# T5-bias attention with a snake MLP: output products and attention numerators in 64-row mode, tail keys by two pairs, one division per pair

## The chip, the core and the metric

The kernel runs on one core of a Trainium2 chip. The core has five engines with queues of their own: PE (TensorE, matmuls), DVE (VectorE), ACT (ScalarE), POOL (GpSimd) and SP (SyncE, which only issues DMAs here). The metric is the time on the device in microseconds (us); less is better.

## What is computed

Eight batches t of eight heads attend over 576 positions of width 64, with a bias that depends on the distance of two positions. The result, 4608 rows of 512, goes through an MLP of width 2048 with a sine in it. The reference, cut to its core:

```python
scores = scale * np.matmul(q, k.transpose(0, 1, 3, 2)) + bias      # (8, 8, 576, 576)
attn = np.exp(scores - max); attn = attn / (attn.sum(-1) + 1e-09)
x = np.matmul(attn, v)                                             # -> (4608, 512)
h = x @ w_in; s = np.sin(alpha * h)                                # (4608, 2048)
out = (h + s * s / alpha) @ w_out                                  # (4608, 512)
```

## The kernel before

**Attention.** The heads are taken in pairs p of two, with head a of a pair in partitions 64a to 64a+63, so that a score matmul uses half of PE's rows and the two heads' matmuls, which follow each other, use different halves (the 64-row mode, "rows" in the code). A pair's 576 keys are four chunks ch of 128 and a tail of 64; its 576 queries are five groups j of 128, the last half empty. qk_t (L1063) makes the scores of 256 queries w with two key chunks: four matmuls of 256 columns into two PSUM banks, and exp_u (L1074) turns them into numerators in one 1024-wide activation. qk_x_rows (L1055) does the last 64 queries with the four chunks, in rows; qk_x_full (L1051) and qk_s (L1038) do the tail keys with full 128-row matmuls, through tail (L1026), from a copy of k in which the two heads stand on a diagonal. DVE multiplies the exponentials by exp(bias) near the diagonal (band_t L1086, band_x L1078, band_s L1046).

**Numerators.** av (L1099) multiplies the exponentials by v with a column of ones, in full 128-row mode: for each j one tail matmul of 130 columns for both heads (L1111), then eight of 65 columns (four chunks for each head, L1120). It is called twice for a pair (two j, then three), each time with one bank, and each time norm (L1124) divides: a reciprocal (L1130) and a multiplication (L1131) on DVE. Then the pair's x is transposed, by a DMA on SP (turn_x L1135) or for the first pairs on PE (turn_x_pe L1141).

**The MLP.** It runs in nine blocks of rows. A unit is one block with one of 16 slices f of the width: moe_in (L1151) does four matmuls, moe_sin (L1168) a sine on ACT, moe_sq (L1173) and moe_g (L1176) a square and h + s*s/alpha on DVE. The output products, moe_out (L1192), take 128 rows tau at a time: 16 matmuls of 512 columns in full mode, two to a piece, into one bank; evict (L1201) and store (L1205) follow.

**What sets the order.** The whole order is laid out when the program is built. _graph (L333) makes tasks with an engine, a duration, a priority and what they depend on; _Plan.run (L177) goes through time, gives each free engine the ready task with the lowest priority number, hands out the eight PSUM banks (_Banks.find, L76) and adds 0.096 us (SWITCH, L121) where PE's mode changes between tasks. The program then issues each engine's instructions in the order found. At run time an engine goes through its own list strictly in order and waits at an instruction whose input isn't there. Scores and moe_in stand in one sequence ("big"), which the option ins fills with units; OPT holds these options, priorities p_... and buffer counts.

## Time and profile before

| | before |
|---|---|
| median of 2 runs | 396.99 us (394.71 and 399.26) |
| span of the profiled execution | 391.7 us |
| PE busy | 374.0 us (95%) |
| DVE busy | 301.1 us (77%) |
| ACT busy | 279.8 us (71%) |
| POOL busy | 86.4 us (22%) |

The profile doesn't say which of the runs it comes from. Its span runs from the first to the last instruction; the lower of the two times is 3.0 us above it and the upper one 7.6 us. "PE" in the profile is matmuls, "PEld" the loads of their stationary operand, which go on beside them. A matmul's row gives its start and its whole duration; since matmuls follow each other before the last one has ended, what one costs is read from start to start, or from the chain of waits, whose pieces follow each other without overlap.

### The profile page before, as it was taken

The numbers are of one execution on the slowest core, as the hardware profiler recorded it, in microseconds if no ns is written. First come the engines' busy times: TensorE is split into PE (matmuls) and PEld (weight loads), VectorE is DVE, ScalarE is ACT, GpSimd is POOL, SyncE is SP. The second block draws the span as 40 slices with busy tenths as digits, with TensorE's granted clock in tenths as the row PEclk, the third lists the DMA queues.
The fourth block names the chain that finished last, engine by engine and source line by source line (L and its number), as shares of the span: only waits on it lengthen the run. The fifth ranks groups of instructions, "written<-read, shape, count | busy, mean of one in ns | idle before, by whom it ended". The sixth has DMA issues, their size and how long they took to land.

```text
span 391.7 us, 9363 instructions
## 1 busy us (share of the span) xinstructions
PE 374.0 (95%) x3811; PEld 201.1 (51%) x3811; DVE 301.1 (77%) x738; ACT 279.8 (71%) x339; POOL 86.4 (22%) x101
## 2 busy tenths in 40 slices
PE   3979979999999999999999999999999999999996
PEld 2557435565446545564466445644664454444442
DVE  6498797777987798769976997798669889778221
ACT  2888876989689978887789769987897964333000
POOL 8695744080008000900080004000000000000000
PEclk9999998999999999999999999999999999999999
DMA  9999999999549924997499329600211001101122
GB/s 165 197 170 183 195 184 149 145 170 165 82 97 168 176 14 91 165 167 57 89 179 153 34 66 204 74 19 28 64 44 42 30 19 46 36 27 56 54 82 80
DMA packets 148171, 40.80 MB, mean 104 GB/s; under 512 B 134416, under 2 KB 143456, under 8 KB 148128
## 3 DMA queue, kind: packets, MB, share of 16 engines
q0 software_dynamic: 96656, 18.45, 57.7%
q1 hardware_dynamic: 50912, 21.25, 27.9%
q8 instruction: 30, 0.49, 0.5%
q10 hardware_dynamic: 560, 0.50, 0.4%
q14 instruction: 13, 0.11, 0.1%
HBM read 36.94 MB, written 15.93 MB: 135 GB/s over the span
## 4 chain that ended last, share of the span: by engine, by line
PE 88%; DVE 8%; DMA 2%; ACT 1%; issue 1%; SPq 0%
PE acc L1197 33%; PE acc L1163 29%; PE acc L1120 9%; PE acc L1069 9%; DVE g L1188 3%; PE acc L1111 2%; PE acc L1030 2%; PE acc L1059 2%; DMA toep<-in_k_dram 2%; DVE u L1097 1%; DVE s L1174 1%; PE acc L1010 1%; PE acc L1035 1%; DVE xp L1131 1%; DVE qT L1020 1%
## 5 line engine op out<-in xcount | busy, mean ns | idle before, releaser
L1076 ACT ACTIVATE u<-acc 128x1024 f16<-128x1024 f32 x160 | 154.4, 1024 | 21.2 <-PE acc L1069 9.7
L1197 PE MATMUL acc<-w_out,g 128*128 128x512 f16 x576 | 142.9, 381 | 0.0
L1163 PE MATMUL acc<-xT,w_in 128*128 128x512 f16 (+2 forms) x640 | 131.5, 358 | 0.0
L1170 ACT ACTIVATE s<-acc,alphaT 128x512 f16<-128x512 f32 (+2 forms) x144 | 96.2, 687 | 48.5 <-DVE g L1188 26.7
L1188 DVE SCALAR_TENSOR_TENSOR g<-s,inv_a,acc 128x512 f16<-128x512 f16 (+4 forms) x176 | 106.1, 643 | 1.6
L1163 PEld LDWEIGHTS <-w_in 128*128 128x128 f16 x640 | 58.8, 98 | 66.6 <-DVE g L1188 1.4
L1197 PEld LDWEIGHTS <-g 128*128 128x128 f16 x576 | 50.1, 98 | 56.0 <-issue 9.2
L1097 DVE TENSOR_TENSOR u<-u,toep 128x256 f16<-128x256 f16 (+1 forms) x128 | 61.0, 489 | 19.2 <-ACT u L1076 19.0
L1174 DVE TENSOR_TENSOR s<-s 128x512 f16<-128x512 f16 (+2 forms) x144 | 55.5, 417 | 6.1 <-ACT s L1170 6.1
L890 POOL DMA_DIRECT2D v<-in_v_dram x32 | 28.4, 900 | 143.6 <-PE acc L1120 135.8
L1120 PE MATMUL acc<-v,u 128*128 128x65 f16 x1280 | 54.6, 193 | 1.2 <-DVE u L1097 1.2
L1120 PEld LDWEIGHTS <-u 128*128 128x128 f16 x1280 | 50.0, 97 | 5.5 <-DVE u L1097 1.7
L1069 PE MATMUL acc<-qT,kT 64*128 64x256 f16 x512 | 45.1, 280 | 2.4 <-DVE g L1188 1.9
L1203 DVE COPY outs<-acc 128x512 f32<-128x512 f32 x36 | 24.7, 687 | 22.6 <-PE acc L1197 22.3
L1131 DVE TENSOR_TENSOR xp<-acc,rden 128x256 f16<-128x256 f32 (+1 forms) x64 | 31.4, 491 | 2.4 <-DVE rden L1130 0.3
L1069 PEld LDWEIGHTS <-kT 64*128 64x128 f16 x512 | 19.1, 96 | 24.6 <-issue 21.7
L1130 DVE RECIPROCAL rden<-acc 128x4 f32<-128x4 f32 (+1 forms) x64 | 12.0, 187 | 21.5 <-PE acc L1120 21.1
L1111 PE MATMUL acc<-vt,u 128*128 128x130 f16 x128 | 28.2, 221 | 0.0
L1111 PEld LDWEIGHTS <-u 128*128 128x128 f16 x128 | 12.5, 97 | 5.9 <-issue 2.1
L911 POOL DMA_DIRECT2D staged_q<-in_q_dram x5 | 13.9, 2783 | 0.0
L911 POOL DMA_DIRECT2D staged_k<-in_k_dram x6 | 13.6, 2259 | 0.7 <-DMA xT<-in_q_dram 0.7
L1059 PE MATMUL acc<-qT,kT 64*128 64x64 f16 x256 | 9.6, 195 | 2.8 <-ACT u L1076 0.9
(61 smaller groups left out, 166.6 us busy)
## 6 DMA issues: line engine op xcount, KB each, us to landing
out_dram<-outs SPq DMA_DIRECT2D x36, 256.0 KB, 2.0
v<-in_v_dram POOLq DMA_DIRECT2D x32, 128.0 KB, 6.7
staged_k<-in_k_dram POOLq DMA_DIRECT2D x6, 576.0 KB, 11.4
staged_q<-in_q_dram POOLq DMA_DIRECT2D x5, 576.0 KB, 15.4
w_in<-in_moe_w_in_dram POOLq DMA_DIRECT2D x4, 512.0 KB, 8.8
w_out<-in_moe_w_out_dram POOLq DMA_DIRECT2D x4, 512.0 KB, 9.6
xT<-in_q_dram POOLq DMA_DIRECT2D x11, 144.0 KB, 7.0
xT<-in_k_dram POOLq DMA_DIRECT2D x7, 144.0 KB, 6.2
```

Source lines behind the costliest of these rows:

```text
L890: self.nc.gpsimd.dma_start(out=self.vs[t % 2][:, c, :, 0:D], in_=src)
L1069: self.nc.tensor.matmul(out=s[:, o:o + 256], lhsT=self.kT[t % 2][r, p, 128 * c:128 * c + 128], rhs=self.qT[t % 2][r, p, 256 * w:256 * w + ...
L1076: self.nc.scalar.activation(out=c["u"], in_=c["s"], func=AF.Exp, scale=0.125)
L1097: self.nc.vector.tensor_tensor(out=io, in0=io, in1=m, op=ALU.mult)
L1111: nc.tensor.matmul(out=c["av"][:, 130 * j:130 * j + 130], lhsT=tail, rhs=vt[:, p, :], start=True, stop=True, skip_group_check=True)
L1120: nc.tensor.matmul(out=c["av"][:, 130 * j + 65 * a:130 * j + 65 * a + 65], lhsT=l, rhs=vv[:, ch, 2 * p + a, 0:65], start=False, stop=True, ...
L1131: self.nc.vector.tensor_tensor(out=self.ap(x, 256 * w, [[64, n], [1, 64]]), in0=self.ap(av, 0, [[65, n], [1, 64]]), in1=self.ap(r, 0, [[1, ...
L1163: self.nc.tensor.matmul(out=c["h"][:, x:y], lhsT=self.w_in[:, j, 128 * f:128 * f + 128], rhs=self.xT[:, j, lo + x:lo + y], start=(j == 0), ...
L1170: self.nc.scalar.activation(out=c["s"], in_=c["h"], func=AF.Sin, scale=self.alphaT[:, f:f + 1])
L1174: self.nc.vector.tensor_tensor(out=c["s"], in0=c["s"], in1=c["s"], op=ALU.mult)
L1188: self.nc.vector.scalar_tensor_tensor(out=o, in0=c["s"][:, x:y], scalar=self.inv_a[:, f:f + 1], in1=c["h"][:, x:y], op0=ALU.mult, op1=ALU.add)
L1197: self.nc.tensor.matmul(out=c["mo"], lhsT=self.g[b][:, f, 128 * (tau % 4):128 * (tau % 4) + 128], rhs=self.w_out[:, f, :], start=(f == 0), ...
```

## The change

- **Numerators** (batches 2 to 7): a pair's five j are done by one set of tasks into two banks, one for each head. If PE is in 64-row mode when the first piece comes, each 128-row matmul is cut into two of 64 rows (av_rows). In turn 0, head 0 takes the first 64 partitions (keys) of each chunk and head 1 the last 64; in turn 1 the halves are swapped. Between the turns stands touch, a DVE copy of one element from each of the two banks: it reads after the last matmul of turn 0 and turn 1 waits for it. If PE is in full mode, the pieces are done in full mode without a touch.
- **Output products**: two groups of 128 rows are taken together, into two banks; each slice f is done in full mode or as two half matmuls with the turns, whichever mode PE is in, and a touch stands between the turns there too. An odd group is done alone in full mode.
- **Tail keys and last queries**: the tail keys of two pairs make one tile (L, four a batch becoming two) of full-mode matmuls of 512 columns; the last queries of two pairs make one tile (R) in rows; each has one band multiplication.
- **Division**: one reciprocal and one multiplication for each pair (norm_pair) instead of two each.
- **Planner and options**: a task may have a gate, which settles its mode and duration when it is chosen. Scores of batches 2 to 7 get two pairs of banks (low=4) in place of three, in a written order for each batch. Priorities, load order, the place of the first MLP units (ins) and buffer counts are new. One more pair is transposed on PE. Batches 0 and 1 keep the old functions for scores and numerators.

The core of the diff:

```diff
+                    if t.gate is not None:
+                        x = t.gate(mode.get(e), None)
+                        if x is None:
+                            continue
+                        r = max(r, x[0] + self.HOP)
+                        t.dur, t.m_in = x[1:3]
+                        t.m_out = t.m_in
...
+    def touch(a, bank):
+        x = add("DVE", 0.07, lambda: K.touch(bank()), deps=[a], prio=opt["p_touch"], name="touch")
+        return x
...
+        if kind == "R":
+            need = [x[t][p] for p in ps for x in (T_k, T_q)]
+            b = feed_one(c, 0.23, "rows", need, lambda s: K.qk_r(s, t, i), 0.92, rr,
+                     lambda: K.exp_r(c), f"R{t}.{i}", [last_qk[t]])
+            c["done"] = add("DVE", 0.25, lambda: K.band_r(c, i), deps=[b] + [T_j[p] for p in ps],
...
+            b = feed_one(c, 0.43, m, need, lambda s: K.qk_tail(s, t, i), 0.92, tr,
+                     lambda: K.exp_u(c, "ut"), f"L{t}.{i}", [last_qk[t]], low=opt["low_t"])
...
+    def close(t, p):
+        tiles = [cells[t, ("T", p, w, h)] for w in range(2) for h in range(2)]
+        cr, ct, cs = cells[t, ("R", p // 2)], cells[t, ("L", p // 2)], cells[t, ("S",)]
+        xcell, acell, xu, users = {}, {}, [], []
+        deps = [c["done"] for c in tiles + [cr, ct, cs]] + T_v[t]
+        first = last = None
+        how = []
+        told = []
+        def gate(mode, task, turn, js):
+            kind = how[0] if how else "rows" if mode == "rows" else "full"
+            if kind == "full" and turn:
+                return 0.0, 0.0, None
+            if turn and told[0].end is None:
+                return None
+            if task is not None:
+                if not how:
+                    how.append(kind)
+                task.emit = lambda: K.av_rows(acell, tag(first), tiles, cr, ct, t, p,
+                                              turn if kind == "rows" else None, js)
+            n = len(js) * (0.295 if kind == "full" else 0.148 - 0.03 * turn)
+            return told[0].end if turn else 0.0, n, kind
+        for turn in range(2):
+            for js in opt["js"]:
+                a = add("PE", len(js) * 0.15, lambda: None, deps=deps, prio=opt["p_av"] - 0.1 * turn,
+                        take=[] if first else [(2, users)], mode="rows", name=f"av{t}.{p}.{turn}")
+                first = first or a
+                a.gate = lambda mode, task, turn=turn, js=js: gate(mode, task, turn, js)
+                deps = [a]
+                last = a
+            if not turn:
+                told.append(touch(last, lambda: tag(first)))
+                told[0].gate = lambda mode, task: (0.0, 0.07 if how[0] == "rows" else 0.0, None)
+                told[0].emit = lambda: K.touch(tag(first)) if how[0] == "rows" else None
+        for c in tiles + [cr, ct, cs]:
+            c["users"].append(last)
+        last_av[t].append(last)
+        nm = add("DVE", 0.95, lambda: K.norm_pair(acell, xcell), deps=[last], prio=opt["p_norm"],
+                 take=[(xr, xu)])
+        users.append(nm)
+        turn_x = x_pe if (t, p) in opt["x_pe"] else x_dma
+        T_x[t][p] = turn_x(t, p, xcell, xu, [nm])
...
+    def moe_out(taus):
+        bs = [b for b in range(len(BLK))
+              if BLK[b][0] < 128 * taus[-1] + 128 and BLK[b][1] > 128 * taus[0]]
+        n = len(taus)
+        done = {"full": 0, 0: 0, 1: 0, "any": False}
+        told = []
+        def gate(mode, task):
+            left = [NF - done["full"] - done[k] for k in range(2)]
+            if not left[1] or n == 1 and not left[0]:
+                return 0.0, 0.0, None
+            turn = int(not left[0])
+            rows = n == 2 and (mode == "rows" or turn)
+            if turn and told[0].end is None:
+                return None
+            at = told[0].end if turn else 0.0
+            k = min(2, left[turn]) if rows else 1
+            if task is not None:
+                if rows:
+                    fs, kind = range(done[turn], done[turn] + k), turn
+                    done[turn] += k
+                else:
+                    fs, kind = range(NF - 1 - done["full"], NF - done["full"]), None
+                    done["full"] += 1
+                    if n == 1:
+                        done[0] = done[1] = 0
+                began, done["any"] = done["any"], True
+                task.emit = lambda: K.moe_out(cell, taus, fs, kind, not began)
+                if n == 2 and NF == done["full"] + done[0] and not told[0].deps:
+                    told[0].deps.append(task)
+                    told[0].prio = opt["p_touch"]
+            return at, 0.2158 * (k if rows else n), "rows" if rows else "full"
+        if n == 2:
+            def tell(mode, task):
+                return (0.0, 0.07 if done[0] else 0.0, None) if told[0].deps else None
+            told.append(add("DVE", 0.07, lambda: K.touch(cell["bank"]) if done[0] else None, name="touch"))
+            told[0].gate = tell
...
 OPT = dict(
+    c_act=((1, 1),), h_act=(), p_bias=1.23, nu=10, nr=2, nl=3, ng=3, first=(1, 1, 1), bs=2,
+    win=6, hold={}, low=4, low_t=4, rows={0: 16, 1: 8, 2: 0}, p_touch=-4.64, js=((0, 1), (2,),
+    (3, 4)), order={-1: _order("L0 001 000 L1 S R0 010 011 100 101 201 R1 111 200 110 210 211 3"), 3: _order("L0 L1 S R0 0 100 101 110 R1 111 201 200 210 211 3"), 5: _order("L0 L1 S R0 000 010 001 011 1 R1 2 301 300 310 311"), 6: _order("L0 L1 R0 000 001 S 010 101 011 100 110 200 111 201 R1 210 211 3"), 7: _order("L0 L1 S R0 000 001 100 010 011 111 101 110 R1 2 301 300 310 311"), 4: _order("S L0 L1 R0 0 1 R1 200 201 310 210 211 300 311 301"), 2: _order("L0 L1 S R0 0 110 101 100 111 R1 201 210 200 301 211 300 310 311")}, new=2, stick=0,
+    single=True, p_bs=0.99, ins={-1: {17: 16}, 0: {}, 1: {9: 16}, 2: {16: 16}, 7: {9: 16}, 5:
+    {16: 16}, 6: {15: 3, 17: 13}, 3: {16: 16}}, s_at={0: 10, 1: 8}, blk=(512, 512, 512, 512,
+    512, 512, 480, 480, 576), p_av=0.06, p_mo=2.37, p_in=2.17, p_band=1.87, p_norm=-0.75,
+    p_sq=2.73, p_g=-1.78, p_ev=0.43, turn_act=(0, 1), x_pe=((0, 0), (0, 1), (0, 2), (0, 3), (1,
+    1)), late=0.0, p_t1=(-1.46, 3.69), act1=((1, 0), (1, 1), (2, 0), (3, 0)), fill=0, nat2=(1,),
+    early=('X0.0', 'T0.0', 'X0.1', 'T0.1'), gq="n01 n10 n03 v0 n02 b1 b3 i0 m0 i1 m1 m3 i2 m2 n13 n12 n11 o0 v1 o1 i3 o2 s20 n20 s21 n21 n23 o3 v2 n22".split())
...
+    def touch(self, bank):
+        self.nc.vector.tensor_copy(out=self.touched, in_=self.acc[0:1, bank:bank + 2, 0])
...
+    def qk_tail(self, s, t, i):
+        for p in range(2):
+            self.tail(s, 512 * p, 512, t, 2 * i + p, 0)
+    def qk_r(self, s, t, i):
+        for p in range(2 * i, 2 * i + 2):
+            for c in range(4):
+                for a in range(2):
+                    r = slice(64 * a, 64 * a + 64)
+                    o = 512 * a + 256 * (p % 2) + 64 * c
+                    self.nc.tensor.matmul(out=s[:, o:o + 64],
+                                          lhsT=self.kT[t % 2][r, p, 128 * c:128 * c + 128],
+                                          rhs=self.qT[t % 2][r, p, 512:576], start=True, stop=True)
+    def exp_r(self, c):
+        c["u"] = self.ur[self.n_r % len(self.ur)]
+        self.n_r += 1
+        self.nc.scalar.activation(out=c["u"][:, 0:1024], in_=c["s"], func=AF.Exp, scale=0.125)
+    def band_r(self, c, i):
+        io = self.ap(c["u"], 192, [[256, 2], [512, 2], [1, 64]])
+        m = self.toep[:, 4 * i:4 * i + 4, 256:320].rearrange("k (p a) n -> k p a n", p=2)
+        self.nc.vector.tensor_tensor(out=io, in0=io, in1=m, op=ALU.mult)
+    def band_tail(self, c, i):
+        io = self.ap(c["u"], 384, [[512, 2], [1, 128]])
+        self.nc.vector.tensor_tensor(out=io, in0=io, in1=self.mt[:, 2 * i:2 * i + 2, 0:128],
+                                     op=ALU.mult)
...
+    def av_rows(self, c, bank, tiles, cr, ct, t, p, turn, js):
+        nc = self.nc
+        c["av"] = self.acc[:, bank:bank + 2, 0:325]
+        vv, vt = self.vs[t % 2], self.vt[t % 2]
+        ul, us, ur = ct["u"], self.us[t % 2], cr["u"]
+        for j in js:
+            w, o = divmod(128 * j, 256)
+            at = slice(65 * j, 65 * j + 65)
+            if turn != 1:
+                for a in range(2):
+                    r = slice(0, 128) if turn is None else slice(64 * a, 64 * a + 64)
+                    l = us[r, 64 * p:64 * p + 128]
+                    if j < 4:
+                        x = 512 * (p % 2) + 128 * j
+                        l = ul[r, x:x + 128]
+                    nc.tensor.matmul(out=c["av"][:, a, at], lhsT=l, rhs=vt[r, p, 65 * a:65 * a + 65],
+                                     start=not j, stop=True, skip_group_check=True)
+            for ch in range(4):
+                for a in range(2):
+                    r = slice(0, 128)
+                    if turn is not None:
+                        r = slice(64 * (a ^ turn), 64 * (a ^ turn) + 64)
+                    if j < 4:
+                        x = 512 * a + 256 * (1 - ch % 2) + o
+                        l = tiles[2 * w + ch // 2]["u"][r, x:x + 128]
+                    else:
+                        x = 512 * a + 256 * (p % 2) + 64 * ch
+                        l = ur[r, x:x + 128]
+                    nc.tensor.matmul(out=c["av"][:, a, at], lhsT=l, rhs=vv[r, ch, 2 * p + a, 0:65],
+                                     start=False, stop=True, skip_group_check=True)
+    def norm_pair(self, c, xcell):
+        xcell["x"] = x = self.tp.tile([128, 5, 128], F16, name="xp", tag="xp", bufs=3)
+        r = self.tp.tile([128, 2, 5], F32, name="rden", tag="rden", bufs=4)
+        av = c["av"].rearrange("s a (j d) -> s a j d", j=5)
+        self.nc.vector.reciprocal(out=r, in_=av[:, :, :, 64])
+        self.nc.vector.tensor_tensor(
+            out=x[:, :, :].rearrange("s j (a d) -> s a j d", a=2), in0=av[:, :, :, 0:64],
+            in1=self.ap(r, 0, [[5, 2], [1, 5], [0, 64]]), op=ALU.mult)
...
+    def moe_out(self, c, taus, fs, turn, first):
+        if first:
+            c["bank"] = c["task"].got[0]
+            c["mo"] = [self.acc[:, c["bank"] + i, :] for i in range(len(taus))]
         for f in fs:
+            for i, tau in enumerate(taus):
+                r = slice(0, 128) if turn is None else slice(64 * (i ^ turn), 64 * (i ^ turn) + 64)
+                at = 128 * (tau % 4)
+                self.nc.tensor.matmul(out=c["mo"][i], lhsT=self.g[tau // 4][r, f, at:at + 128],
+                                      rhs=self.w_out[r, f, :], start=first and f == fs[0],
+                                      stop=True, skip_group_check=True)
```

More of the change, by code (lines that the diff above doesn't have):

```diff
@@ L87, in find @@
         else:
-            for i in range(6 if low else 8):
+            for i in range(low):
                 if at[i] is None:
@@ L114, in __init__ @@
         self.wait = 0.0
+        self.low = 8
+        self.gate = None
         self.got = []
@@ new lines, in element @@
+    def element(t):
+        order = opt["order"].get(t, opt["order"][-1])
+        closed = 0
+        for what in order:
+            score(t, what)
+            while closed < NP and all((t, x) in cells for x in
+                                      [("T", closed, w, h) for w in range(2) for h in range(2)]
+                                      + [("R", closed // 2), ("L", closed // 2), ("S",)]):
+                close(t, closed)
+                closed += 1
+            yield
+        assert closed == NP
@@ L688, in moe_out @@
+        if n == 2:
[3 more added lines that the diff above has]
+            told[0].gate = tell
+        for piece in range(NF + (n == 2)):
+            deps = list(T_wout)
             for b in bs:
-                deps += [G_done[b][f] for f in fs]
-                if not piece and not early:
+                if not piece:
@@ L705, in moe_out @@
+            m.gate = gate
+            j = opt["hold"].get((state["j"], piece))
+            if j is not None and bs[-1] + 1 < NBLK - 1:
+                held.setdefault((bs[-1] + 1, j), []).append(m)
+            if piece == 0:
+                cell["task"] = m
             last = m
         state["mo"] = last
-        g_users.setdefault(tau // 4, []).append(last)
-        ou = []
-        ev = add("DVE", 0.61, lambda: K.evict(cell), deps=[last], prio=opt["p_ev"], take=[(outr, ou)])
-        users.append(ev)
```

160 lines of the change are left out of this document (110 added, 50 removed).

## The prediction

> **What bounds the kernel.** I read first how much each engine works, then the same by stretches of the span, to see whether one engine is the limit everywhere.
>
> ```profile
> span 391.7 us, 9363 instructions
> PE 374.0 (95%) x3811; PEld 201.1 (51%) x3811; DVE 301.1 (77%) x738; ACT 279.8 (71%) x339; POOL 86.4 (22%) x101
> PE 88%; DVE 8%; DMA 2%; ACT 1%; issue 1%; SPq 0%
> ```
>
> ```profile
> core 0: us, PE busy (x) PEld busy (x) DVE busy (x) ACT busy (x) POOL busy (x), PEclk, DMA share, GB/s
> 20.00:40.00 20.00, 16.10 (x366) 12.49 (x366) 17.73 (x53) 17.56 (x22) 15.49 (x25) 1.00 1.44 178
> 40.00:60.00 20.00, 17.83 (x143) 8.72 (x144) 18.02 (x39) 16.30 (x22) 11.65 (x13) 0.98 1.58 185
> 60.00:100.00 40.00, 39.50 (x552) 23.70 (x552) 30.15 (x83) 34.00 (x41) 12.30 (x10) 0.96 1.82 156
> 100.00:140.00 40.00, 40.00 (x414) 20.91 (x412) 33.32 (x81) 33.80 (x41) 9.26 (x8) 1.00 1.17 125
> 220.00:260.00 40.00, 40.00 (x396) 20.87 (x394) 33.50 (x80) 32.99 (x40) 4.78 (x6) 1.00 0.63 88
> 300.00:340.00 40.00, 40.00 (x255) 19.08 (x254) 36.19 (x90) 25.89 (x34) 0.00 (x0) 1.00 0.10 31
> ```
>
> From 100 us on PE has no gap (40.00 of 40.00), while DVE and ACT work 33 to 36 of 40. So there the time is the sum of what PE does, and a saving on PE counts in full as long as nothing new makes PE wait. Only before 60 us does PE stand still (3.9 and 2.2 us in the two stretches of 20).
>
> A busy PE may still spend time on changes of mode. Those show in the chain of waits, whose pieces don't overlap:
>
> ```profile
> 189.33 1.29 PE acc L1197 x6
> ...
> 191.17 2.59 PE acc L1197 x12
> ...
> 202.32 1.40 PE acc L1197 x6
> 203.72 0.32 PE acc L1069 x4
> 204.05 0.12 PE acc L1059 x8
> 204.16 0.33 PE acc L1030 x2
> 204.49 0.06 PE acc L1111
> 204.54 0.24 PE acc L1120 x8
> 204.78 0.06 PE acc L1111
> 204.84 0.24 PE acc L1120 x8
> ```
>
> Six output products that follow full-mode work take 1.29 us (0.216 each; twelve take 2.59). The six at 202.32 follow 64-row scores and take 1.40: the change of mode costs about 0.10 us. The other way it costs the same: four 64-row score matmuls take 0.32 here, and rows further down give four without one 0.22.
>
> **The change, part by part.**
>
> *Changes of mode.* I counted them in the issue order of the two compiled programs, by the rows and columns of the array that each matmul uses: 201 before, 126 after. 75 fewer at 0.097 us (0.10 as read above, 0.11 for the row 1.40 against 1.29) are -7.3 us. They lie in the saturated part, so this counts in full.
>
> *Numerators.* A j in full mode is 0.06 + 0.24 = 0.30 us above. In the new order 80 of the 120 j of batches 2 to 7 are in rows (16 pairs), 40 in full mode, and the 40 of batches 0 and 1 are as before. A row-mode j is 18 matmuls of 65 columns, nine couples on opposite halves of the array. The nearest row is the eight of 64 columns on L1059: 0.12 us, so four couples at 0.029. Nine are 0.26 us. The gain is that the tail's 130 columns, of which half multiply zeros, become one couple. 80 x 0.037 = -2.9 us. The 40 in full mode have two tail matmuls of 65 in place of one of 130: nothing, since L1120 costs 0.24/8 = 0.030 each.
>
> *Output products.* 236 stay in full mode, 340 become 680 half matmuls, 340 couples. Nothing, if a couple of 512 columns takes what a full one takes. The rows for that:
>
> ```profile
> 201.71 0.61 PE L1069 MATMUL acc<-qT,kT 64*128 64x256 f16 x8
> 202.25 1.47 PE L1197 MATMUL acc<-w_out,g 128*128 128x512 f16 x6
> 203.66 0.39 PE L1069 MATMUL acc<-qT,kT 64*128 64x256 f16 x4
> 203.88 0.28 PE L1059 MATMUL acc<-qT,kT 64*128 64x64 f16 x8
> ```
>
> From start to start, four of 256 columns take 203.88 - 203.66 = 0.22 us, two couples at 0.11, half of the 0.216 of 512 columns. So halves run side by side at no loss.
>
> *Other PE work.* Tail scores keep their columns (24 matmuls of 512 for 48 of 256), last queries too. One more pair is transposed on PE, five at about 0.055: +0.3 us, and one DMA less on SP.
>
> *DVE.* Its rows:
>
> ```profile
> L1188 DVE SCALAR_TENSOR_TENSOR g<-s,inv_a,acc 128x512 f16<-128x512 f16 x112 | 79.4, 739 | 0.2
> L1131 DVE TENSOR_TENSOR xp<-acc,rden 128x384 f16<-128x384 f32 x32 | 17.8, 557 | 1.1
> L1131 DVE TENSOR_TENSOR xp<-acc,rden 128x256 f16<-128x256 f32 x32 | 13.6, 424 | 1.3 <-DVE rden L1130 0.3
> L1130 DVE RECIPROCAL rden<-acc 128x6 f32<-128x6 f32 x32 | 6.2, 193 | 10.0 <-PE acc L1120 9.7
> L1081 DVE TENSOR_TENSOR u<-u,toep 128x128 f16<-128x128 f16 x32 | 7.0, 217 | 3.6 <-ACT u L1076 3.6
> L974 DVE COPY alphaT<-acc 128x16 f32<-128x16 f32 x1 | 0.2, 164 | 0.0
> ```
>
> For 24 pairs one reciprocal in place of two saves 24 x 0.19 = 4.6 us; one multiplication of 640 (0.82, by the slope from 256 to 384) in place of 0.42 + 0.56 saves 3.8. 48 band multiplications of 0.217 (10.4 us) become 24 of 256 elements (6.9, estimated at the 0.29 that twice the width would add to), saving 3.5. 29 touches at the 0.164 of the small copy out of PSUM cost 4.8. In all -7 of 301 us, off the path: nothing. What covers this is DVE's free 6 to 7 us in each 40; where it has least, 36.19 of 40, hardly any touch stands.
>
> *The touch as a wait.* PE's second turn can't start before turn 0 has ended on PE, DVE has come to the touch, made it, and told PE. The rows for that way:
>
> ```profile
> 63.33 0.41 PE L1120 MATMUL acc<-v,u 128*128 128x65 f16 x8
> 63.78 0.18 DVE L1130 RECIPROCAL rden<-acc 128x4 f32<-128x4 f32 x1 [0.91 <-PE acc L1120]
> ```
>
> The last of these matmuls starts near 63.33 + 7 x 0.03 = 63.54 and ends at 63.74, DVE starts at 63.78. With 0.164 for the copy and again 0.04 back, a turn is 0.45 us from the last start to the release, if DVE is free; if it has just begun a 0.74 us operation, 1.2. PE has other work there. In the issue order ten of the 16 numerator turns have four half output products and one score tile between them (0.43 + 0.22 = 0.65 us), six over 1 us; of the 13 turns of output products three have one score tile (0.22), four two tiles (0.44), six over 1. Below: 3 x 0.23 = 0.7 us of standing still. Above, with DVE always just begun: 10 x 0.55 + 3 x 0.98 + 4 x 0.76 + 6 x 0.15 = 12 us. DVE is at work 83% of the time and half an operation is 0.35 us, so a turn waits 0.3 more on average: 0.1 for each of the ten, 0.5 for the three and 0.3 for the four, 3.7 in all; but the touch has DVE's best priority and the order puts the second turn behind it. I take +2.3 us, in the middle between 0.7 and 3.7. On DVE itself the touch holds up what is queued behind it, band multiplications and g, by the 0.25 us that turn 0 needs to end: 29 x 0.25 = 7 us of idle, which DVE has.
>
> *The stretch before 60 us.* These are its rows:
>
> ```profile
> 40.00 0.27 PE L1059 MATMUL acc<-qT,kT 64*128 64x64 f16 x7 [0.94 <-DVE xT L1148]
> 58.26 0.39 PE L1069 MATMUL acc<-qT,kT 64*128 64x256 f16 x4 [1.59 <-DVE g L1188]
> 61.45 1.04 PE L1197 MATMUL acc<-w_out,g 128*128 128x512 f16 x2
> L1076 ACT ACTIVATE u<-acc 128x1024 f16<-128x1024 f32 x160 | 154.4, 1024 | 21.2 <-PE acc L1069 9.7 <-PE acc L1030 5.8 <-PE acc L1035 3.6
> ```
>
> PE waits until the first MLP block is through DVE; the first output product starts at 61.45, and from then on PE is full. In the new order 30 j instead of 22 stand ahead of it: 8 x 0.30 = 2.4 us of work that moves into time in which PE waited anyway. But three more score tiles stand there too, 3 x 1.02 us on an ACT that is nearly full there (17.56 and 16.30 of 20). So between -2.4 and +0.7; I take -1.5, nearer the gain, as ACT has 6 us free in the two rows.
>
> *Sum.* -7.3 - 2.9 + 0.3 - 1.5 + 2.3 = -9.1 us. The span goes from 391.7 to 382.6, and the median, which stands 5.3 us above the span, from 397.0 to 388.
>
> **A rule that speaks against it.** The row first: eight matmuls of 64 columns on L1059 took 0.12 us, 0.015 each. The Trainium skill ("TensorE: Matmul & The Clock Gate", part 1) says that the distance from one matmul's start to the next never falls below about 25 ns, however few columns it has. By that a row-mode j would take 18 x 0.025 = 0.45 us instead of 0.26, an estimate from that page: 80 x 0.19 = +15 us, and the 192 matmuls of the last queries at 0.010 more each add 2, so the time would be about 405. The trace disagrees for eight in a row, so the sum goes by 0.029 a couple; the first rival below holds what is left of it.
>
> **Rivals.**
>
> *The couples don't last* (ends slower). The trace has eight short row-mode matmuls in a run; the new order has 50 and then 40, each with a weight load of its own. If PE can't be fed that fast, each takes up to the 0.030 of a full-mode one: 1440 x 0.0155 = +22 us, and the 192 of the last queries +3: 397 - 9 + 25 = 413. It decides from 0.021 us each, where the gain is gone; at 0.026 it is 2% slower (397 - 9.1 + 1440 x 0.0118 = 405). For it: no row shows more than eight. Against: L1059 shows no slowing within the eight. 399 to 413.
>
> *PE waits instead of changing.* The two banks for numerators and two for output products leave the scores two pairs of banks for three, so a score tile must wait for the exponential two before it (1.02 us), and the turns may wait as worked out above. With 12 us of turns in place of 2.3, or 0.08 us at each of the 120 wide tiles of batches 2 to 7, the gain is gone: 391 to 399. For it: a turn can't be made up for by running ahead. Against: PE stood idle nowhere after 100 us with an order made in the same way, and ACT has 6 us in 40 free.
>
> *The change isn't made.* PE's mode decides at each piece, so changes could have stayed; the count of 126 rules this out.
>
> **How the numbers follow.** My forecast, 382 to 391 with 388 the likeliest, 0.62. Waits instead, 391 to 399, 0.20. Couples that don't last, 399 to 413, 0.14. Better than 382 (no turn waits, the whole early gain), 0.04. About 2% (8 us) is what a measurement here can tell from no change. Faster than 389 is most of the first case and the last one: 0.50. Slower than 405 is the upper part of the couples' case and something unforeseen: 0.13. Between: 0.37. The range from 381 to 400 leaves out the couples' case and a little below.
>
> **What would show it.** Right: the four pieces of 0.32, 1.40 and 0.33 in the chain become 0.22, 1.29 and 0.22 where output products stand among scores; a turn of 50 in the timeline starts and ends within 0.73 us, and one of 40 within 0.58; PE is at 40.00 of 40 after 100 us; the row of the small DVE copy has 29 instructions near 0.16 us, and waits of PE for it under 0.2. Wrong: row-mode numerators over 0.02 us each from start to start; PE idle at turns or at scores, released by DVE or ACT; first output products later than 62 us. A steady saving below 8 us with PE still full would mean that I misread the price of a mode change.

## The result, and the profile after

| | before | after |
|---|---|---|
| median of 2 runs | 396.99 us (394.71 to 399.26) | 415.75 us (415.09 to 416.42) |
| span of the profiled execution | 391.7 us | 414.3 us |
| PE busy | 374.0 us (95%) | 379.9 us (92%) |

The changed kernel takes 1.049 times as long (95% interval 1.037 to 1.062), 18.8 us more, where 9.1 less was forecast. The two profiled executions are 22.6 us apart; single executions lie up to some 3 us from their kernel's median (spans of before, run again beside the experiments, were 392.7 to 396.2 us), so differences of that size between two profiles say little. From the page after:

```profile
span 414.3 us, 11467 instructions
PE 379.9 (92%) x4892; PEld 211.3 (51%) x4892; DVE 300.3 (72%) x698; ACT 281.4 (68%) x339; POOL 86.6 (21%) x101
...
PE 56%; DVE 24%; DMA 8%; ACT 5%; issue 4%; POOL 2%; SPq 0%; DVEq 0%; ACTq 0%
```

PE was 88% of the chain that ended last, with 8% of DVE beside it. Now it is 56%, DVE is 24%, and "issue", time in which an engine waited for nothing that the profile shows, is 4%. By stretches:

```profile
40.00:60.00 20.00, 16.72 (x207) 10.50 (x208) 12.49 (x34) 15.80 (x19) 11.50 (x14) 0.83 1.70 187
60.00:100.00 40.00, 36.53 (x501) 19.54 (x501) 29.39 (x71) 30.12 (x36) 14.02 (x11) 0.96 1.49 131
100.00:140.00 40.00, 33.07 (x512) 18.88 (x510) 29.40 (x67) 30.50 (x38) 4.86 (x7) 0.91 0.90 95
140.00:180.00 40.00, 39.38 (x572) 22.63 (x570) 31.91 (x72) 31.98 (x39) 7.98 (x7) 1.00 1.05 112
180.00:220.00 40.00, 36.88 (x528) 21.34 (x526) 30.87 (x69) 31.39 (x38) 10.94 (x11) 1.00 1.22 113
220.00:260.00 40.00, 37.82 (x530) 20.44 (x528) 29.41 (x63) 29.67 (x36) 5.00 (x4) 0.96 0.96 104
```

PE's 40.00 of 40 is gone from 100 us to 260: 33.07, 39.38, 36.88, 37.82. DVE and ACT do less there than before (29 to 32 of 40, against 32 to 34), so neither has become the bound. Waiting has. The column behind the engines is the granted clock: 0.83 from 40 to 60, 0.91 from 100 to 140. What PE waits for, in us in all, times, and the longest:

```profile
PE acc L1387 <- issue: 6.3, 4, 2.3
...
PE acc L1287 <- ACT u L1295: 4.5, 9, 1.1
PE acc L1287 <- DVE g L1463: 4.2, 3, 1.6
...
PE acc L1277 <- DVE g L1463: 1.4, 1, 1.4
...
PE acc L1476 <- issue: 1.1, 1, 1.1
PE acc L1476 <- DVE touched L1228: 0.9, 3, 0.4
```

L1387 is the row-mode numerators, L1476 the output products, L1287 and L1277 score tiles. 7.4 us are waits on issue, some ten us waits of score tiles for ACT's exponentials and DVE's g, and 1.3 us waits for the touch, 0.4 of them of score tiles. All waits on issue lie behind 100 us, but of the score tiles' only 4.0 us do (2.6 for g, 1.4 for exponentials).

**An account of PE.** Busy time hides this, since a matmul's row lasts longer than the distance to the next one. So I split the time from PE's first matmul to its last in two. Work is what each matmul takes to the next start where nothing disturbs it (0.216 us for 512 columns, 0.109 for a couple of 256, 0.029 for a couple of 65 or a full-mode matmul of 65; a couple is two matmuls on opposite halves), plus 0.096 for each change of mode, counted over the program. The rest is standing still, running at half the clock included. The times are medians; the columns behind them are of the one execution that was profiled.

| kernel | time, us | matmul starts span | work | mode changes | standing still to 100 us | after |
|---|---|---|---|---|---|---|
| before | 396.99 | 383.1 | 360.0 | 201 | 20.4 | 2.7 |
| after | 415.75 | 405.5 | 351.8 | 126 | 29.1 | 24.6 |
| num_full | 414.8 | 403.5 | 356.9 | 160 | 27.9 | 18.7 |
| early_as_before | 414.79 | 403.8 | 350.6 | 118 | 29.8 | 23.4 |
| prio_early | 421.14 | 410.8 | 351.0 | 131 | 29.8 | 30.0 |
| out_single | 410.56 | 399.8 | 365.9 | 263 | 28.0 | 5.9 |
| out_full_same | 442.84 | 430.8 | 356.7 | 183 | 28.0 | 46.1 |
| laid_anew | 404.1 | 390.5 | 350.5 | 114 | 28.0 | 12.0 |
| laid_anew_single | 406.47 | 395.4 | 362.1 | 232 | 27.2 | 6.1 |
| scores_six | 403.37 | 391.9 | 366.5 | 269 | 21.3 | 4.0 |
| scores_four | 404.91 | 394.5 | 367.1 | 275 | 21.4 | 6.0 |

The change takes 8.2 us of work off PE, as forecast, and adds 30.6 us of standing still: 8.7 before 100 us, 21.9 after. That is 22.4 us more, the difference of the two spans in the table. The experiments ask where that comes from. My theory was the order: it makes PE wait for instructions and for other engines at places where the old one didn't. The rivals were that row mode itself is slow, that fewer banks for the scores cost it, and that the late start is carried through to the end.

### The profile page after: what moved, and what is told of

It reads as the page before. It is cut to its first block, busy times and chain, and to the rows that moved or that the text cites. A ratio compares the mean times of both kernels' runs of the same rounds, so it can differ in the third digit from the quotient of the medians.

```text
span 414.3 us, 11467 instructions
## 1 busy us (share of the span) xinstructions
PE 379.9 (92%) x4892; PEld 211.3 (51%) x4892; DVE 300.3 (72%) x698; ACT 281.4 (68%) x339; POOL 86.6 (21%) x101
## 4 chain that ended last, share of the span: by engine, by line
PE 56%; DVE 24%; DMA 8%; ACT 5%; issue 4%; POOL 2%; SPq 0%; DVEq 0%; ACTq 0%
PE acc L1476 24%; DVE g L1463 14%; PE acc L1438 13%; DVE s L1449 7%; PE acc L1387 7%; PE acc L1287 5%; ACT u L1295 3%; DMA w_in<-in_moe_w_in_dram 2%; DMA vt<-in_v_dram 2%; DMA toep<-in_k_dram 2%; DMA kT<-staged_k 2%; PE acc L1234 1%; PE acc L1374 1%; PE acc L1211 1%; DVE outs L1482 1%
## 5 line engine op out<-in xcount | busy, mean ns | idle before, releaser
L1476 PE MATMUL acc<-w_out,g 64*128 64x512 f16 (+1 forms) x916 | 148.5, 380 | 2.9 <-issue 1.1
L1295 ACT ACTIVATE u<-acc 128x1024 f16<-128x1024 f32 x136 | 130.7, 1028 | 24.0 <-PE acc L1287 15.2
L1331 DVE TENSOR_TENSOR u<-u,toep 128x1024 f16<-128x1024 f16 (+1 forms) x128 | 61.8, 493 | 31.3 <-ACT u L1295 30.3
L1476 PEld LDWEIGHTS <-g 64*128 64x128 f16 (+1 forms) x916 | 54.8, 95 | 51.8 <-issue 10.1
L1287 PE MATMUL acc<-qT,kT 64*128 64x256 f16 x512 | 51.9, 290 | 9.2 <-ACT u L1295 4.5
L1387 PE MATMUL acc<-v,u 64*128 64x65 f16 (+1 forms) x1280 | 36.9, 193 | 6.4 <-issue 6.3
L1287 PEld LDWEIGHTS <-kT 64*128 64x128 f16 x512 | 25.9, 98 | 30.6 <-issue 16.6
L1387 PEld LDWEIGHTS <-u 64*128 64x128 f16 (+1 forms) x1280 | 32.0, 96 | 10.3 <-issue 8.8
L1395 DVE TENSOR_TENSOR xp<-acc,rden 128x640 f16<-128x640 f32 x24 | 19.8, 824 | 0.8
L1374 PE MATMUL acc<-vt,ut 64*128 64x65 f16 (+1 forms) x192 | 18.6, 193 | 0.0
L1354 PE MATMUL acc<-v,u 128*128 128x65 f16 x320 | 15.1, 203 | 0.0
L1354 PEld LDWEIGHTS <-u 128*128 128x128 f16 x320 | 14.1, 104 | 0.1
```

What stands on the lines that cost most here:

```text
L1287: self.nc.tensor.matmul(out=s[:, o:o + 256], lhsT=self.kT[t % 2][r, p, 128 * c:128 * c + 128], rhs=self.qT[t % 2][r, p, 256 * w:256 * w + ...
L1295: self.nc.scalar.activation(out=c["u"], in_=c["s"], func=AF.Exp, scale=0.125)
L1331: self.nc.vector.tensor_tensor(out=io, in0=io, in1=m, op=ALU.mult)
L1354: nc.tensor.matmul(out=c["av"][:, 130 * j + 65 * a:130 * j + 65 * a + 65], lhsT=l, rhs=vv[:, ch, 2 * p + a, 0:65], start=False, stop=True, ...
L1387: nc.tensor.matmul(out=c["av"][:, a, at], lhsT=l, rhs=vv[r, ch, 2 * p + a, 0:65], start=False, stop=True, skip_group_check=True)
L1476: self.nc.tensor.matmul(out=c["mo"][i], lhsT=self.g[tau // 4][r, f, at:at + 128], rhs=self.w_out[r, f, :], start=first and f == fs[0], sto ...
```

## The experiments

Times of before, run again beside them, were 395.96 to 396.46 us; ratios are to those.

**num_full: numerators always in full mode, the order kept.**

```diff
-                task.emit = lambda: K.av_rows(acell, tag(first), tiles, cr, ct, t, p,
-                                              turn if kind == "rows" else None, js)
+                task.emit = lambda: None if turn else K.av_rows(acell, tag(first), tiles, cr, ct, t, p, None, js)
...
-                told[0].emit = lambda: K.touch(tag(first)) if how[0] == "rows" else None
+                told[0].emit = lambda: None
```

> The changed kernel with its order of tasks kept, but the numerators of batches 2 to 7 always done in full 128-row mode: the second turns issue nothing and their touches go. Theory 1 (PE runs out of instructions: the changed kernel's PE waited for nothing that the profile shows, four times in numerators, 6.3 us in all, at the moments when a 16 KB instruction packet landed): a pair's numerators are 100 instructions in 1.5 us instead of 180 in 1.3, so these waits go, and with them two stretches of half clock that followed them (about 3 us). Against that stand some 32 changes of mode more (3.1 us) and 80 j at 0.30 instead of 0.26 us (2.9 us). Expected 409 to 413 us, waits of L1387 for issue under 1 us. Theory 2 (the order itself stands still, and the issue waits only show up in time that would be waited anyway): the waits go, but the time rises by the 6 us, to 420 to 423.

414.8 us, ratio 1.047 (1.043 to 1.051): between the two theories. PE's instructions (matmuls and their weight loads) fall from 9784 to 8504. Its waits:

```profile
PE acc L1286 <- ACT u L1294: 4.4, 7, 1.2
PE acc L1190 <- DMA ident<-eye: 4.4, 1, 4.4
PE acc L1286 <- DVE g L1462: 4.2, 3, 1.6
```

No wait on issue is left, while those for ACT and DVE stand as they were. Standing still falls by 7.1 us, work rises by 5.1, so the row-mode numerators lost by waits about what they saved.

**early_as_before: load order, place of the first units, S tiles and p_bias as before.**

```diff
-    p_bias=1.23, ins={... 1: {9: 16} ...}, s_at={0: 10, 1: 8}, gq="n01 n10 n03 v0 ..."
+    p_bias=-0.5, ins={... 1: {5: 16} ...}, s_at={0: 9, 1: 9}, gq="n01 n10 v0 n03 ..."
```

> The changed kernel with the load order, the place of the first MLP units, the places of the two small score tiles and the priority of the bias matmuls as in the kernel before. Theory 1: the first output product, at 73.75 us in the changed kernel against 61.45 before, is late because its loads and first units stand later; with the old ones it comes at 62 to 66, and since PE is nearly full behind it, the time falls by 6 to 9 us, to 407 to 410. Theory 2: the first part is late because of the priorities and the numerators that stand ahead of it, or what it gains is waited for later: 413 to 418.

414.79 us, ratio 1.049 (1.045 to 1.052): no gain, as theory 2 said. The first output product came at 67.2 us instead of 73.8, but the second MLP block's first matmul at 105.9, against 106.6 after and 91.9 before: the early time was lost again before 106 us.

**probe_feed: the kernel before, and behind it 640 couples of 65 columns, then 640 full-mode matmuls of 65.**

```diff
+    def burst(self):
+        for n in range(640):
+            for a in range(2):
+                r = slice(64 * a, 64 * a + 64)
+                self.nc.tensor.matmul(out=self.acc[:, a, 0:65], lhsT=self.blank[r, 0:128],
+                                      rhs=self.blank[r, 0:65], start=True, stop=True)
+        for n in range(640):
+            self.nc.tensor.matmul(out=self.acc[:, 2, 0:65], lhsT=self.blank[:, 0:128],
+                                  rhs=self.blank[:, 0:65], start=True, stop=True)
```

> The kernel before, with matmuls on a blank tile added behind its last output product: 640 couples of 65 columns in 64-row mode, then 640 matmuls of 65 columns in full mode. Theory 1 (PE can be short of instructions, 256 of them to a 16 KB packet): the couples, 4 instructions in 0.029 us, go on for one or two packets (up to some 128 couples) and then stand still at each packet, so that 640 couples take 30 us or more, with waits for issue of 0.5 to 2 us each; the full-mode ones take 640 x 0.030 = 19 us with hardly any. Theory 2 (the waits for issue have another cause): the couples take 640 x 0.029 = 18.6 us without gaps.

From the timeline (start, length, count, and in brackets the idle time before it):

```profile
390.66 3.93 PE L1205 MATMUL acc<-blank 64*128 64x65 f16 x247
395.76 2.12 PE L1205 MATMUL acc<-blank 64*128 64x65 f16 x128 [1.16 <-issue]
399.49 2.12 PE L1205 MATMUL acc<-blank 64*128 64x65 f16 x128 [1.61 <-issue]
...
421.31 2.12 PE L1205 MATMUL acc<-blank 64*128 64x65 f16 x128 [1.61 <-issue]
425.04 0.32 PE L1205 MATMUL acc<-blank 64*128 64x65 f16 x9 [1.61 <-issue]
425.29 19.59 PE L1208 MATMUL acc<-blank 128*128 128x65 f16 x640
```

247 matmuls go at 0.015 us each; then PE stops, and from there gets 128 at a time, with their 128 weight loads 256 instructions, every 3.64 us on average ((421.31 - 399.49) / 6). In full mode one matmul takes 0.03 us, so 256 instructions last 3.9 us and no gap shows. The couples took 34.6 us instead of 18.6.

**probe_feed_loads: the same with 16 loads of v and four stagings on POOL beside it.**

```diff
+        for i in range(4):
+            for c in range(4):
+                self.load_v(7, c)
+            self.stage(7, i % 2)
```

> The same probe with loads of POOL's queue (16 of the v loads and 4 stagings of k and q, all of them repeats) running beside the added matmuls. Theory 1, if the packet of instructions has to pass through the same DMA engines as the loads: the waits at each packet grow against the probe without loads, from 0.5 to 2 us to 2 to 5, and the full-mode matmuls begin to wait too. Theory 2 (loads don't matter): both parts take what they take in the probe without loads.

```profile
399.34 3.28 PE L1210 MATMUL acc<-blank 64*128 64x65 f16 x128 [2.71 <-issue]
405.81 3.44 PE L1210 MATMUL acc<-blank 64*128 64x65 f16 x128 [3.19 <-issue]
412.28 3.60 PE L1210 MATMUL acc<-blank 64*128 64x65 f16 x128 [3.03 <-issue]
```

Beside the loads the same 256 instructions come every 6.47 us; when the loads are over, from 425 us on, every 3.5 to 4.0 again. Each probe is a single run. The page of each kernel has a queue for them, first before, then after:

```profile
q8 instruction: 30, 0.49, 0.5%
```

```profile
q8 instruction: 38, 0.62, 0.6%
```

Packets and MB: 16 KB a packet, 7622 and 9784 PE instructions, about 256 to each. In the kernel after, each of PE's five waits on issue ends 1.2 to 1.6 us after a packet of this queue has landed (102.4 and 103.83, 135.0 and 136.23, and so on). On average 38 packets in 405 us, one in 10.7, are no problem. But two pairs' numerators in rows are 360 instructions in 2.7 us of work, and there what has been fetched is used up. This is how it looks in the kernel after:

```profile
100.64 0.39 PE L1287 MATMUL acc<-qT,kT 64*128 64x256 f16 x4
100.86 0.20 PE L1374 MATMUL acc<-vt,ut 64*128 64x65 f16 x2
...
101.01 0.20 PE L1374 MATMUL acc<-vt,ut 64*128 64x65 f16 x2
...
101.35 0.19 PE L1387 MATMUL acc<-v,u 64*128 64x65 f16 x1
103.83 0.29 PE L1387 MATMUL acc<-v,u 64*128 64x65 f16 x7 [2.29 <-issue]
103.94 0.22 PE L1374 MATMUL acc<-vt,us 64*128 64x65 f16 x2
```

**prio_early: early_as_before, and also the priorities, window and x_pe of before.** The edit is in OPT alone (p_av=0.2, p_mo=1.6, p_in=0.8, p_norm=0.0, win=7 and so on).

> The changed kernel with the priorities, the load order, the place of the first MLP units and the pair transposed on PE as before; the functions, the written order of scores in batches 2 to 7 and the banks stay. Measured so far: the loads alone brought the first output product from 73.8 to 67.2 us and the time by 1 us only, as the second MLP block still began at 105.9 us (106.6 in the changed kernel, 91.9 before). Theory 1 (the first 100 us cost half of the loss, through priorities and loads together): the second block begins by 96 us and the time falls by 7 to 10, to 405 to 409. Theory 2 (the new functions hold more banks, and PE waits for them wherever they stand): the second block begins after 102 us and the time stays within 412 to 420.

421.14 us, ratio 1.063 (1.059 to 1.067): the second block began at 103.75 us, as theory 2 said, but both theories' times were too low. Its largest wait accounts for most of that:

```profile
PE acc L1386 <- issue: 12.2, 7, 3.6
```

It has more row-mode numerators (9950 instructions), and the waits on issue rise by 4.8 us over after's 7.4.

**out_single: each output group alone, in one bank and full mode, the order laid out for that.**

```diff
-                while len(ready) > 1:
-                    moe_out([ready.pop(0), ready.pop(0)])
-                if ready and opt["single"]:
-                    moe_out([ready.pop()])
+                while ready:
+                    moe_out([ready.pop(0)])
```

> The changed kernel with each group of 128 rows of the output products alone, in one bank and in full mode; numerators still in rows where PE is in rows. Instruction order: 263 changes of mode against 126. Theory 2 (two banks for the output products beside two for the numerators leave too few for scores and MLP units): PE's waits for ACT and DVE in front of scores, 4.5 and 4.2 us in the changed kernel, fall to a half, and although 137 changes more cost 13 us, the time rises by 5 or less: 412 to 421. Theory 1 (banks don't matter, the loss is instruction supply and the first 100 us): the time rises by the whole 13 us or so, to 426 to 430.

410.56 us, ratio 1.035 (1.030 to 1.041), below what both theories gave: 14.1 us more work than after, and yet faster. Standing still after 100 us falls from 24.6 to 5.9. Waits of score tiles for g fall too, but there is also no wait on issue, with only six pairs' numerators in rows, so this run doesn't tell banks from instructions:

```profile
100.00:140.00 40.00, 38.82 (x458) 19.85 (x457) 32.92 (x71) 33.92 (x41) 9.22 (x8) 1.00 1.20 116
180.00:220.00 40.00, 39.97 (x478) 20.20 (x471) 31.54 (x69) 32.85 (x40) 10.43 (x9) 1.00 1.09 110
```

**out_full_same: output products always full, but after's order and its two banks kept.**

```diff
-                task.emit = lambda: K.moe_out(cell, taus, fs, kind, not began)
+                task.emit = lambda: None if kind else K.moe_out(cell, taus, fs, None, not began)
```

> The changed kernel with its order of tasks kept, but output products always in full mode: the first turn does both groups for its slices, the second issues nothing, their touches go. 183 changes of mode against 126. If a change costs 0.097 us and couples of 512 columns cost what full matmuls do, the time rises by 57 x 0.097 = 5.5 us less up to 1 us of touches: 419 to 421. If the row mode of output products has a cost of its own, it rises by less than 3: 414 to 418.

442.84 us, ratio 1.119 (1.114 to 1.124), above every forecast. Work is 4.9 us over after, as counted, but all of an output group's work now comes in turn 0 and none in turn 1, and the score tiles wait for ACT more often:

```profile
PE acc L1288 <- ACT u L1296: 12.8, 21, 1.2
PE acc L1288 <- DVE g L1464: 5.9, 5, 1.6
...
PE acc L1235 <- ACT u L1296: 4.2, 7, 1.0
```

So it doesn't price row mode; it shows how much hangs on where work stands in the order: some 20 us more standing still, with 5 us more work.

**laid_anew and laid_anew_single: all parts of the change, another order.** The planner lets no task of PE start before its instructions are there; priorities, written orders and ins were chosen anew with that in it, and numerators come in two pieces instead of three. The second takes each output group alone, in an order of its own.

```diff
+    FEED = ((290.0, 6.5), (1e9, 3.7))
+    AHEAD = 64
+    def supply(self, now, n):
+        while self.fed + n >= 256 * len(self.there):
+            b = len(self.there)
+            asked = max(self.there[b - 1], self.entered(256 * (b - 1) - self.AHEAD))
+            self.there.append(asked + next(x for t, x in self.FEED if asked < t))
+        return self.there[(self.fed + n) // 256]
...
+                    if e == "PE" and t.ins and self.feed:
+                        r = max(r, self.supply(now, t.ins) - (t.dur if t.ins > 16 else 0.0))
```

> The changed kernel with all its parts, only its order laid out anew: the planner also counts PE's instructions (256 to a packet, the next packet asked for when the one before is begun, 6.5 us for a packet while the loads run and 3.7 after) and lets no task start before its packet is there; priorities and the written orders of the batches are others. By the program PE's work is the same as after (350.8 us from start to start without standing still, against 351.8; 114 changes of mode against 126). Theory 1, the time was lost to the order, which asked for instructions faster than they come and bunched scores ahead of busy banks, and not to the 64-row work itself: no waits on issue after 100 us, standing still falls from 54 us to 30 or less, time 392 to 402. Theory 2, the pairs of banks and the turns cost this by themselves in any order: 408 to 416.

> As laid_anew, but each output group alone, in one bank and full mode (232 changes of mode, 362.5 us of PE work without standing still, 11.7 more than laid_anew); numerators in rows where PE is in rows. Theory 1, banks for pairs of output groups aren't what costs once the order fits: slower than laid_anew by 5 to 12, 400 to 408. Theory 2, they are: faster than laid_anew, 398 to 406 with laid_anew at 408 or more.

laid_anew: 404.1 us, ratio 1.020 (1.016 to 1.023). 2 us over theory 1 and below theory 2's range: the same work on PE, 11.7 us less time than after. Its waits:

```profile
PE acc L1411 <- ACT u L1419: 5.7, 10, 1.2
...
PE acc L1511 <- issue: 2.4, 3, 1.3
```

Waits on issue are a third of after's, where theory 1 had none, and standing still after 100 us is half (12.0 against 24.6). The 28.0 us before 100 us hardly moved, so that standing still is 40.0 us in all, not the 30 or less of theory 1; of what the profile shows behind 100 us, 2.4 us are issue, 1.7 touches and 0.7 exponentials. laid_anew_single: 406.47 us, ratio 1.024 (1.018 to 1.029), 2.4 slower than laid_anew with intervals that overlap: less than the 5 to 12 of theory 1, and not faster as in theory 2. By the account it has 11.6 us more work, 5.9 less standing still after 100 us and 0.8 less before, the 4.9 us between the two profiled executions, of which laid_anew's took 400.9 us.

**scores_six and scores_four: the kernel before with scores of batches 2 to 7 issued one tile at a time, in three or in two pairs of banks.**

```diff
-            for i in range(0, 6 if low else 8, 2):
+            for i in range(0, low, 2):
...
-        if len(batch["parts"]) == (...):
-            flush()
+        if name[1] > "1" or len(batch["parts"]) == (...):
+            flush(4 if name[1] > "1" else 6)
```

> The kernel before, scores of batches 2 to 7 issued one tile at a time instead of two, still with three pairs of banks: the control for scores_four. By the program 269 changes of mode against 201, PE work 367.1 us against 360.0: time 402 to 406 if PE stays full.

> As scores_six, but the score tiles of batches 2 to 7 may use only two pairs of banks, as in the changed kernel (275 changes, 367.6 us of PE work). Theory 1, two pairs for the scores make PE wait for the exponentials: 8 us or more over scores_six, waits of score tiles for ACT of 6 us or more. Theory 2, two pairs are enough by themselves: within 3 us of scores_six.

403.37 us, ratio 1.018 (1.014 to 1.022), within its forecast, and 404.91 us, 1.023 (1.018 to 1.028), as theory 2 said. The first prices a change of mode by itself: 68 more are 6.5 us of work, and the time rose by 7.1. The second is 1.5 us above the first, so two pairs of banks for the scores hardly cost by themselves, in a kernel whose numerators and output groups take one bank each.

## Why the prediction was wrong

**Changes of mode, -7.3: right.** Work fell by 75 x 0.096 = 7.2 us, and scores_six shows that such work counts in full where PE doesn't stand still. The row at 100.64 above has four scores in 0.22 us before numerators in rows, not the 0.32 of a change.

**Numerators and turning, -2.6: the sign right, the size somewhat too large.** By the account, work other than mode changes fell by 1.0 us. Read from starts, a j in rows takes 0.15 us in turn 0 (100.86 to 101.01 above) and 0.12 in turn 1, together 0.27 where I had 0.26: 80 x 0.03 = 2.4 us, less the 0.3 for the pair more on PE. So the saving lies between 1.0 and 2.1. The timeline of after, further down, has the turn of 40 from 332.96 to 333.56:

```profile
332.96 0.65 PE L1387 MATMUL acc<-v,u 64*128 64x65 f16 x32
333.44 0.29 PE L1387 MATMUL acc<-v,ur 64*128 64x65 f16 x8
333.56 0.60 PE L1476 MATMUL acc<-w_out,g 64*128 64x512 f16 x4
```

0.60 us for 20 couples, 0.030 each; the forecast was 0.58.

**Turns, +2.3: right in kind.** PE waited 1.3 us for touches, near the lower bound of 0.7, though up to 0.4 at once, not under 0.2. The touch costs DVE 0.14 us each, its idle before it is in its row:

```profile
L1228 DVE COPY touched<-acc 1x2 f32<-1x2 f32 x29 | 4.2, 143 | 7.8 <-PE acc L1387 6.3 <-PE acc L1476 1.3
```

7.8 us against 7 forecast.

**Early stretch, -1.5: wrong, +8.7.** I took three more score tiles and eight more j ahead of the first MLP block as filling for time in which PE waited. The first output product came at 73.8 us, not at 61.4, and PE now stands still 29.1 us before 100, not 20.4. Of the 8.7 more, the waits that the profile shows are about 3 (17 against 14), and half clock, 10.2 us long against 3.4, is another 3 or so. Some of the waits, in its timeline:

```profile
40.87 0.61 PE L1287 MATMUL acc<-qT,kT 64*128 64x256 f16 x8 [0.88 <-ACT u L1295]
...
44.12 0.44 PE L1419 MATMUL acc<-ident,xp 128*128 128x128 f16 x5 [0.81 <-DVE xp L1406]
...
46.14 0.23 PE L1345 MATMUL acc<-vt,u 128*128 128x130 f16 x1 [0.76 <-DMA vt<-in_v_dram]
```

The scores wait for exponentials, x for its division, the numerators of batch 1 for v; after these three the clock is at half from 46.6 to 53.4 us. Which move in the order does it isn't settled: early_as_before and prio_early undid the ones that I thought of, with 29.8 us each, and laid_anew kept 28.0. It isn't the scores' banks: in after, the wide score tiles of batch 2, the first batch with two pairs, start at 90.9 us only.

**The step that failed** is "a saving on PE counts in full as long as nothing new makes PE wait", with the reason given against the second rival, that PE stood idle nowhere after 100 us with an order made in the same way. The forecast had 2.3 us for turns and nothing for any other wait. The new order did make PE wait, 21.9 us more after 100. The trace shows where most of it stands. Waits on issue, which come when 256 instructions are used up faster than the next arrive, are 7.4 us. Three stretches of half clock, 3.4 us each, cost about 5 us; two of them follow waits on issue, one waits for g. Waits for other engines behind 100 us, of which before had none, are 6.0: 2.9 for g, 1.4 for exponentials, 1.0 for touches, 0.7 for a division. That leaves some 3.5 us which no row shows. num_full took the waits on issue away, and 5.9 us of the standing still after 100. What another order regains is shown only in sum: 5.9 us of standing still are left in out_single, 12.0 in laid_anew. Laid_anew_single has 5.9 less than laid_anew, but the two differ in order as well as in the output groups' banks. So how much of the waiting for g and exponentials is due to held banks stays open.

**The first rival, couples that don't last, named the resource and priced it wrongly.** It had each couple slow down from 0.029 to 0.060. Couples keep 0.030 until what has been fetched is used up, then PE stops, for 0.7 to 2.3 us in after and up to 3.6 in prio_early. So the cost hangs on how they are bunched and not on their count alone: 7.4 us with 16 pairs' numerators in rows in after, 12.2 with 18 in prio_early, 2.4 with 13 in laid_anew. By the rule that I weighed ("TensorE: Matmul & The Clock Gate", part 1, in the Trainium skill), starts never less than 25 ns apart, the 247 in probe_feed would take 6.2 us; they started within 3.93. In a burst the rule doesn't hold for couples. Over many packets the probe's mean is above it, 3.64/128 = 28 ns, for another reason.

**The second rival, PE waits instead of changing,** came nearest in kind, but its range of 391 to 399 was too low. It priced only turns and score banks, and these cost less than it allowed, 1.3 us and, in scores_four, 1.5; the waiting came elsewhere.

Against before, laid_anew has 9.5 us less work, 7.6 more standing still up to 100 us and 9.3 more after. So with the best order here the work saved and the standing still added behind 100 us cancel, within the 3 us that such sums can be off, and what is left of the loss is the early stretch. No version beat the kernel before. Whether an order can keep PE full under this change stays open.

## What to carry to other kernels

A saving worked out on a full engine is only worth what the new order leaves of it: say for each place at which work is moved what arrives there last, and count waiting as its own term, since busy time doesn't show it. Splitting a matmul into two halves at the same array time doubles its instructions, so count instructions in the densest few us against what can be fetched there, not over the whole kernel. A saving by fewer changes of mode is real (0.096 us each), but waiting that a new order brings can cost more.

## What the runs showed of the chip

PE's instructions came in 16 KB packets of about 256, every 3.64 us on average with little else on the DMA engines and every 6.47 beside POOL's loads; 640 full-mode matmuls, which use 256 instructions in 3.9 us, showed no stop. And half clock followed short waits: after the 2.29 us at 101.5 to 103.8, the clock was granted at half for 3.4 us.

```profile
104.60:108.00 3.40, 3.40 (x52) 1.92 (x49) 1.78 (x5) 2.28 (x3) 0.00 (x0) 0.50 2.08 157
```

The window of 3413 ns that the Trainium skill gives ("TensorE: Matmul & The Clock Gate", part 1) agrees with the length. It asks for an idle window of about 3.4 us ahead of it; the longest wait behind 100 us in after was 2.29 us, and twice, at 70.7 and 73.3 us and at 122.2 and 124.2, half clock followed two waits of 1.0 to 1.6 us that ended within 3 us of each other. The length of the waits alone doesn't settle it: in probe_feed nine waits of 1.2 to 1.9 us, one every 3.6 us, left the clock at full.
